# A multimodal attention block: the first block's scale as a column from TensorE, reordered transposes, and output tiles of 512, 512 and 128 columns

## Chip, core and metric

The kernel runs on one core of a Trainium2 chip. Its time is device microseconds of one execution, and lower is better. The profile is one execution taken by the hardware profiler; its times count from the start of the span.

## The reference, cut to what matters

```python
mod_i = (silu(c) @ wmod_img).reshape(B, 6, 1, D)       # B 2, D 1152
shi, sci, gai = mod_i[:, 0], mod_i[:, 1], mod_i[:, 2]
hi = layernorm(x_img) * (1 + sci) + shi                # x_img (2, 256, 1152)
qkvi = hi @ wqkv_img
...                                                    # the same for 32 text tokens per batch
p = softmax(einsum('bqd,bkd->bqk', q, k) * D ** -0.5)  # text and image tokens together
out_i = x_img + gai * ((p @ v)[:, Nt:] @ wo_img)
out_t = x_txt + gat * ((p @ v)[:, :Nt] @ wo_txt)
```

The first matrix product that keeps TensorE busy for long is V of the image. It needs the normalised image, transposed, times the scale column (1 + sci) of each block of 128 features. So four things must be there before it starts: the image, the scale weight (2.65 MB), the transposes, and the first piece of the V weight.

## The kernel before: the parts concerned

The scale is computed as rows: the scale weight is the moving operand, and `silu(c)` is loaded as 32 weight columns at four places of the array. VectorE then transposes the result to columns (`sc_cols`). The transposed image goes through PSUM tiles `tp`, three blocks each; ACT (ScalarE) or VectorE copies them out. `mm` and `tr` are TensorE's product and transpose, and `pin` keeps an instruction at its place in program order.

```python
ps_mm = tile_pool(name="ps_mm", bufs=6, space=PSUM)
ps_tr = tile_pool(name="ps_tr", bufs=2, space=PSUM)
...
def x_transposes(k0, b):
    tr_pool = b == 1 or k0 < 6                  # b 0, k0 6 takes a tile of ps_mm
    tp = (ps_tr if tr_pool else ps_mm).tile([P, 3, NI], bf, ...)
    for kt in range(k0, k0 + 3):
        for t in range(TPB):                    # TPB 2: the two token tiles of a batch
            i = b * TPB + t
            tr(tp[:, kt - k0, t * P:(t + 1) * P], xn_i[:, i, kt * P:(kt + 1) * P], ident[:])
    ...                                         # returns the copy to xT_i: VectorE for k0 3, else ACT
...
for out in [x_transposes(k0, 0) for k0 in (0, 3, 6)]:
    out()
sc_rows(0, 4)                                   # first piece of the scale weight
warm_up(3)
sc_rows(4, 7)                                   # second piece
out01 = x_transposes(0, 1)
out31 = x_transposes(3, 1)
sc_rows(7, K8)                                  # third and fourth pieces
sc_rows(K8, KT)
out61 = x_transposes(6, 1)
out01()
sc_cols(0, 1)                                   # VectorE: rows to a column
x_scale(0, 1, 0, step=1)                        # VectorE: first scaled block
sc_cols(1, 5)
x_scale(1, 3, 0)
v_open(A0, 0, 3)                                # V begins
...
def out_img(i, chunks, parts=None, between=None):
    for n in chunks:                            # (384, 384, 384); last tile (384, 384, 224, 160)
        if c0 and between: between = between()  # tile 1: the text gate, after its first chunk
        ...                                     # nine products of n columns
        nc.vector.tensor_mul(tmp[:, 0:n], ps[:, 0:n], gb[:, b, c0:c0 + n])
        nc.vector.tensor_add(o[:, c0:c0 + n], tmp[:, 0:n], x_i[:, i, c0:c0 + n])
```

Of the kernel before, what the change touches and what calls it, by code (L numbers as in the profile page):

```python
# [14 lines left out]
def kernel(  # L15
# [14 lines left out]
    nc = tc.nc  # L30
    bf = mybir.dt.bfloat16
    f32 = mybir.dt.float32
    PSUM = bass.MemoryType.PSUM

    B, NI, D = x_img.shape
    NT = x_txt.shape[1]
    P = 128
    KT = D // P
    NTOK = NI + NT
    NIT = (B * NI) // P  # L40
    TPB = NI // P
    NTT = B * NT
    CH = 384
    NCH = D // CH
    VC = 288
# [7 lines left out]
    work = ctx.enter_context(tc.tile_pool(name="work", bufs=2))  # L53
    small = ctx.enter_context(tc.tile_pool(name="small", bufs=4))
    ps_mm = ctx.enter_context(tc.tile_pool(name="ps_mm", bufs=6, space=PSUM))
    ps_tr = ctx.enter_context(tc.tile_pool(name="ps_tr", bufs=2, space=PSUM))

    pin = tc.keep_in_program_order

    def mm(*a, **k):  # L60
        return pin(nc.tensor.matmul(*a, **k))  # L61

    def tr(*a, **k):
        return pin(nc.tensor.transpose(*a, **k))  # L64
# [6 lines left out]
    x_i = act.tile([P, NIT, D], bf)  # L71
# [4 lines left out]
    def wtile(slot):  # L76
        return wpool.tile([P, KT, D], bf, tag="w%d" % slot, name="t")
# [4 lines left out]
    K8 = KT - 1  # L82
# [17 lines left out]
    w_sc_i = wtile(0)  # L100
# [21 lines left out]
    warm = const.tile([P, 512], bf)  # L122
# [3 lines left out]
    unit = const.tile([P, LW], bf)  # L126
# [5 lines left out]
    def warm_up(n):  # L132
        for _ in range(n):
            mm(wps[:], lhsT=warm[:, 0:P], rhs=warm[:], start=True, stop=True)
# [33 lines left out]
    sT = const.tile([P, KT, B], bf)  # L168
# [42 lines left out]
    def ln_norm(x_ap, mean, rstd, np_, out_ap):  # L211
        pin(nc.vector.tensor_scalar(out_ap, x_ap, mean, rstd[0:np_, :], op0=ALU.subtract, op1=ALU.mult))

    xn_i = act.tile([P, NIT, D], bf, tag="A")
    hS_i = act.tile([P, KT, B * NI], bf, tag="Bt")
    xT_i = act.tile([P, KT, B * NI], bf)
# [3 lines left out]
    def group(w, kt, g):  # L220
        return w[:, kt, :].rearrange("p (c g l) -> p g c l", g=NGG, l=LW)[:, g]

    def mod_cols_of(gps, name):
        t = const.tile([P, KT, LW], f32, name=name, tag={"sctc": "shc"}.get(name, name))
        pin(nc.vector.transpose(t[:].rearrange("p c l -> p (c l)"), gps[:].rearrange("p c l -> p (c l)")))
        return t

    sc_ps = ps_mm.tile([P, KT, LW], f32, tag="mm")

    def sc_rows(r0, r1):  # L230
        if r0 == 0:
            for g in range(NGG):
                mm(sc_ps[LW * g:LW * g + LW].rearrange("p c l -> p (c l)"), lhsT=unit[:], rhs=warm[:, 0:KT * LW],
                   start=True, stop=False, tile_position=(0, LW * g))
        for kt in range(r0, r1):
            for g in range(NGG):
                mm(sc_ps[LW * g:LW * g + LW], lhsT=sT32[:, kt, :], rhs=group(w_sc_i, kt, g),
                   start=False, stop=(kt == KT - 1), tile_position=(0, LW * g))

    def x_transposes(k0, b):  # L240
        tr_pool = b == 1 or k0 < 6
        tp = (ps_tr if tr_pool else ps_mm).tile([P, 3, NI], bf, tag="tr" if tr_pool else "mm", name="tp")
        for kt in range(k0, k0 + 3):
            for t in range(TPB):
                i = b * TPB + t
                tr(tp[:, kt - k0, t * P:(t + 1) * P], xn_i[:, i, kt * P:(kt + 1) * P], ident[:])
        dst = xT_i[:, k0:k0 + 3, b * NI:(b + 1) * NI]

        def copy_out():
            pin(nc.vector.tensor_copy(dst, tp[:]) if k0 == 3 else nc.scalar.copy(dst, tp[:]))  # L250

        return copy_out

    sc1_i = const.tile([P, KT, LW], f32, name="scc", tag="scc")

    def sc_cols(c0, c1):
        pin(nc.vector.transpose(sc1_i[:, c0:c1, :].rearrange("p c l -> p (c l)"),
                                sc_ps[:, c0:c1, :].rearrange("p c l -> p (c l)")))

    def x_scale(k0, k1, b, step=TPB):  # L260
        for kt in range(k0, k1):
            for t in range(0, TPB, step):
                t0, t1 = b * NI + t * P, b * NI + (t + step) * P
                pin(nc.vector.tensor_scalar(hS_i[:, kt, t0:t1], xT_i[:, kt, t0:t1], sc1_i[:, kt, b:b + 1], None,  # L264
                                            op0=ALU.mult))

    VW = 512
# [3 lines left out]
    def v_open(ids, k0, k1, kt_major=True):  # L271
        for key in ids:
            if key not in accs:
                accs[key] = ps_mm.tile([P, VW], f32, tag="mm", name="vps")
        loop = [(kt, key) for kt in range(k0, k1) for key in ids] if kt_major else \
            [(kt, key) for key in ids for kt in range(k0, k1)]
        for kt, (i, cc) in loop:
            mm(accs[(i, cc)][:], lhsT=hS_i[:, kt, i * P:(i + 1) * P], rhs=w_v_i[:, kt, cc * VW:(cc + 1) * VW],
               start=(kt == 0), stop=(kt == KT - 1), skip_group_check=True)
            if kt == KT - 1:  # L280
                evac(v_i[:, i, cc * VW:(cc + 1) * VW], accs[(i, cc)][:])
# [18 lines left out]
    r3, r2 = ln_rstd(m3[:, 1:2], P), ln_rstd(s2[:, 2:3], P, sign=-1.0)  # L300
    ln_norm(x_i[:, 3, :], m3[:, 0:1], r3, P, xn_i[:, 3, :])
    ln_norm(x_i[:, 2, :], s2[:, 0:1], r2, P, xn_i[:, 2, :])
    for out in [x_transposes(k0, 0) for k0 in (0, 3, 6)]:
        out()
    sc_rows(0, 4)
    warm_up(3)
    sc_rows(4, 7)
    out01 = x_transposes(0, 1)
    out31 = x_transposes(3, 1)
    sc_rows(7, K8)  # L310
    sc_rows(K8, KT)
    out61 = x_transposes(6, 1)
    out01()
    sc_cols(0, 1)
    x_scale(0, 1, 0, step=1)
    sc_cols(1, 5)
    x_scale(1, 3, 0)
    v_open(A0, 0, 3)
    out31()
    out61()  # L320
    x_scale(0, 3, 1)
    sc_cols(5, KT)
    for k0 in (3, 6):
# [200 lines left out]
    gb = act.tile([P, B, D], bf, tag="Bt")  # L524
    gbf = act.tile([P, 2, VC], bf)
    xf = act.tile([P, 2, VC], bf)
# [112 lines left out]
    def attn_pair(ids0, ids1):  # L639
        t0 = {key: ps_mm.tile([P, NTOK], f32, tag="mm", name="aps") for key in ids0}  # L640
        attn_keys(t0, True)
        t1 = {key: ps_mm.tile([P, NTOK], f32, tag="mm", name="aps") for key in ids1}
        for n, key in enumerate([x for pair in zip(t0, t1) for x in pair]):
            first, (b, dt) = key in t1, key
            r0, vcols = v_txt_cols(b, dt)
            mm((t1 if first else t0)[key][:], lhsT=vcols,
               rhs=pTs[b][r0:r0 + NT, 2, :], start=first, stop=not first, tile_position=(r0, 0))
        attn_evac(t0)
        attn_keys(t1, False)
        attn_evac(t1)  # L650
# [34 lines left out]
    for dts in ((0, 5, 1), (6, 2, 7), (3, 8, 4)):  # L685
        attn_pair(*[[(b, dt) for dt in dts] for b in range(B)])

    def out_img(i, chunks, parts=None, between=None):
        b = i // TPB
        t0 = b * NTOK + qpos[b][i % TPB]  # L690
        o = work.tile([P, D], bf, tag="o")
        c0 = s0 = 0
        for n in chunks:
            if c0 and between:
                between = between()
            ps = ps_mm.tile([P, CH], f32, tag="mm")
            for dt in range(KT):
                mm(ps[:, 0:n], lhsT=aT[:, dt, t0:t0 + P], rhs=w_o_i[:, dt, c0:c0 + n],
                   start=(dt == 0), stop=(dt == KT - 1))
            tmp = work.tile([P, CH], bf, tag="tmp")  # L700
            nc.vector.tensor_mul(tmp[:, 0:n], ps[:, 0:n], gb[:, b, c0:c0 + n])  # L701
            nc.vector.tensor_add(o[:, c0:c0 + n], tmp[:, 0:n], x_i[:, i, c0:c0 + n])  # L702
            c0 += n
            if parts is None and c0 == D or parts and c0 in parts:
                (nc.scalar if parts and c0 == D else nc.sync).dma_start(oi_v[b, i % TPB, :, s0:c0], o[:, s0:c0])
                s0 = c0

    def out_txt():
        of = work.tile([P, 2, VC], bf, tag="of", bufs=1)
        for r in range(2):  # L710
            ps = ps_mm.tile([P, VC], f32, tag="mm")
            for dt in range(KT):
                for g in range(2):
                    c0 = (2 * r + g) * VC
                    mm(ps[64 * g:64 * g + NTT, :], lhsT=aT[:, dt, NI:NI + NTT], rhs=w_o_t[:, dt, c0:c0 + VC],
                       start=(dt == 0), stop=(dt == KT - 1), tile_position=(0, 64 * g))
            tmp = work.tile([P, CH], bf, tag="tmp")
            nc.vector.tensor_mul(tmp[:, 0:VC], ps[:], gbf[:, r, :])
            nc.vector.tensor_add(of[:, r, :], tmp[:, 0:VC], xf[:, r, :])
        for g in range(2):  # L720
            eng = nc.sync if g == 0 else nc.scalar
            eng.dma_start(ot_flat.rearrange("t (r g j) -> g t r j", r=2, g=2)[g], of[64 * g:64 * g + NTT, :, :])

    C3 = (CH, CH, CH)
    out_img(0, C3)
    out_img(1, C3, between=txt_gate)
    out_img(2, C3)
    out_txt()
    out_img(3, (CH, CH, 224, 160), parts=(2 * CH, D - 160, D))


# [28 lines left out]
```

## Time and profile before

| | before |
|---|---|
| time, median of 3 runs | 118.11 us (117.92 to 118.4) |
| TensorE busy, share of the span | 95% |
| first product of the second scale piece | 11.70 us |
| first V product | 14.15 us |
| last VectorE addition starts | 113.27 us |

The last two rows are read from the chain in order of time; the stretch between them is 99.12 us and holds nearly nothing but TensorE. What can be changed at the start lies ahead of 14.15 us. The prediction shows the lines for it. Three more are of use. Two are from the timeline of TensorE: start, length, what, count.

```profile
12.96 0.51 PE L61 MATMUL sc_ps<-t,sT 128*32 128x288 bf16 x8
13.58 0.49 PE L64 MATMUL tp<-ident,xn_i 128*128 128x128 bf16 x6
```

The last six transposes begin at 13.58 because their tile is the one that ACT empties until 13.53. The third is from VectorE's timeline near the end; the bracket is the idle time ahead and what ended it.

```profile
108.43 0.46 DVE L718 TENSOR_TENSOR tmp<-ps,gbf 128x288 bf16<-128x288 f32 x1 [1.41 <-PE ps L61]
```

This is the text output times its gate `gbf`, which comes through a small round trip to memory.

### The profile page before, as it was taken

The page shows a single profiled execution, that of the slowest core. Times are in us where ns is not written, and L with a number is a line of the kernel's source. Part 1 is how long each engine was busy: PE and PEld are TensorE (multiplying, and loading weights), DVE is VectorE, ACT ScalarE, POOL GpSimd, SP SyncE. Part 2 cuts the span into 40 slices and gives each one's busy share as a digit, 9 for nine tenths or more (in the row PEclk, how much of TensorE's full clock was granted, in tenths as well). Part 3 has the DMA queues.
Part 4 walks back from the last instruction along what each step waited for, and adds up shares of the span by engine and source line. Part 5 has one row for each costly group of instructions (what it writes and reads, how often), then busy time and mean ns, then how long its engine had stood idle before and what let it go on. Part 6 is the DMA issues. An engine that isn't in the chain of part 4 may idle for free.

```text
span 116.0 us, 2561 instructions
## 1 busy us (share of the span) xinstructions
PE 110.5 (95%) x1064; PEld 63.6 (55%) x1072; DVE 72.2 (62%) x153; ACT 44.3 (38%) x92; POOL 12.4 (11%) x34
## 2 busy tenths in 40 slices
PE   4999999999999999999999999999999999999990
PEld 1246644445674444444454457887866565566670
DVE  3478594062869999999995040018758508566571
ACT  4799710041752298725241233244657400100000
POOL 7300000000000000000000000003440700407000
PEclk9999999999999999999999999999999999999999
DMA  3999999999999999999999999999999999931323
GB/s 111 373 373 404 406 405 408 416 411 408 416 398 408 319 408 410 405 412 412 411 340 412 412 412 414 402 416 400 412 403 409 409 415 366 363 139 37 116 51 102
DMA packets 18917, 41.02 MB, mean 354 GB/s; under 512 B 1323, under 2 KB 1851, under 8 KB 18907
## 3 DMA queue, kind: packets, MB, share of 16 engines
q1 hardware_dynamic: 18032, 39.85, 89.4%
q0 software_dynamic: 480, 0.89, 2.3%
q10 hardware_dynamic: 395, 0.12, 0.4%
q8 instruction: 8, 0.13, 0.4%
q14 instruction: 2, 0.02, 0.0%
HBM read 39.52 MB, written 1.34 MB: 352 GB/s over the span
## 4 chain that ended last, share of the span: by engine, by line
PE 84%; DMA 8%; DVE 2%; SPq 1%; issue 1%; ACT 1%; DVEq 0%
PE ps L61 52%; PE vps L61 15%; DMA t<-in_wmod_img_dram 8%; PE gps L61 5%; PE aps L61 5%; PE sps L61 4%; DVE tmp L701 1%; PE sc_ps L61 1%; DVE o L702 1%; SPq L104 1%; PE tp L64 1%; ACT pT L621 1%; PE pT_ps L64 0%; SPq L108 0%; PE tpt L64 0%
## 5 line engine op out<-in xcount | busy, mean ns | idle before, releaser
L61 PE MATMUL ps<-xT_i,t 128*128 128x512 bf16 x157 | 35.4, 379 | 0.3
L61 PEld LDWEIGHTS <-t 128*128 128x128 bf16 x324 | 20.5, 98 | 19.0 <-issue 0.5
L435 DVE SCALAR_TENSOR_TENSOR acc_sh<-t,sTf,acc_sh 128x1152 f32<-128x1152 bf16 x16 | 21.4, 1404 | 0.0
L61 PE MATMUL ps<-t,aT 128*128 128x384 bf16 (+3 forms) x153 | 20.3, 308 | 0.0
L61 PE MATMUL vps<-t,hS_i 128*128 128x512 bf16 (+1 forms) x106 | 17.8, 325 | 0.2
L61 PEld LDWEIGHTS <-aT 128*128 128x128 bf16 (+1 forms) x153 | 13.0, 101 | 7.1 <-issue 0.8
L61 PEld LDWEIGHTS <-hS_i 128*128 128x128 bf16 x108 | 9.0, 98 | 8.7 <-DVE hS_i L264 0.4
L365 ACT CAST qkT<-ps 128x512 bf16<-128x512 f32 (+2 forms) x11 | 6.1, 551 | 15.0 <-PE ps L61 13.6
L701 DVE TENSOR_TENSOR tmp<-ps,gb 128x384 bf16<-128x384 f32 (+2 forms) x13 | 6.8, 524 | 7.2 <-DMA gb<-mod_scratch 3.8
L587 POOL TENSOR_SCALAR pb<-e,rs 128x32 bf16<-128x32 f32 (+1 forms) x5 | 2.2, 445 | 76.0 <-DVE rs L584 76.0
L61 PE MATMUL wps<-warm 128*128 128x512 bf16 x24 | 8.1, 499 | 1.6 <-DVE unit L127 1.5
L363 ACT ACTIVATE qkT<-ps 128x512 bf16<-128x512 f32 (+2 forms) x11 | 6.1, 561 | 8.6 <-PE ps L61 8.5
L180 DVE CAST v_i<-vps 128x512 bf16<-128x512 f32 x5 | 3.5, 691 | 7.5 <-PE vps L61 7.5
L572 DVE TENSOR_REDUCE nmx<-sps 128x1 f32<-128x288 f32 x4 | 1.8, 458 | 9.5 <-PE sps L61 9.5
L182 ACT CAST v_i<-vps 128x512 bf16<-128x512 f32 x4 | 2.3, 580 | 9.9 <-PE vps L61 9.9
L61 PEld LDWEIGHTS <-sT 128*32 128x32 bf16 x180 | 4.6, 96 | 2.4 <-issue 1.8
L61 PEld LDWEIGHTS <-warm 128*128 128x128 bf16 x25 | 2.7, 118 | 5.5 <-issue 3.0
L634 DVE TENSOR_SCALAR aT<-aps,svc 128x288 bf16<-128x288 f32 x9 | 4.3, 518 | 2.2 <-PE aps L61 2.2
L61 PE MATMUL sps<-qkT 128*128 128x288 bf16 (+1 forms) x54 | 5.3, 287 | 0.0
L61 PE MATMUL gps<-t,sT 128*32 128x288 bf16 x144 | 5.2, 287 | 0.0
L61 PE MATMUL ps<-hT_t,t 128*128 128x64 bf16 x162 | 5.2, 193 | 0.0
L61 PE MATMUL aps<-pT,v_i 128*128 128x288 bf16 x36 | 5.1, 287 | 0.1
(111 smaller groups left out, 105.3 us busy)
## 6 DMA issues: line engine op xcount, KB each, us to landing
t<-in_wqkv_txt_dram SPq DMA_DIRECT2D x3, 2592.0 KB, 19.1
t<-in_wmod_img_dram SPq DMA_DIRECT2D x2, 2592.0 KB, 14.1
t<-in_wmod_txt_dram SPq DMA_DIRECT2D x2, 2592.0 KB, 18.1
t<-in_wqkv_img_dram SPq DMA_DIRECT2D x3, 864.0 KB, 14.0
t<-in_wqkv_img_dram SPq DMA_DIRECT2D x1, 2592.0 KB
t<-in_wo_img_dram SPq DMA_DIRECT2D x3, 864.0 KB, 9.8
t<-in_wqkv_img_dram SPq DMA_DIRECT2D x3, 576.0 KB, 10.0
t<-in_wmod_txt_dram SPq DMA_DIRECT2D x2, 864.0 KB, 13.1
```

The costliest lines, as they stand in the source:

```text
L61: return pin(nc.tensor.matmul(*a, **k))
L64: return pin(nc.tensor.transpose(*a, **k))
L104: nc.sync.dma_start(x_i[:, b * TPB:(b + 1) * TPB, :], x_img[b].rearrange("(p t) d -> p t d", t=TPB))
L180: nc.vector.tensor_copy(out_ap, in_ap)
L182: nc.scalar.copy(out_ap, in_ap)
L363: nc.scalar.mul(out_ap, in_ap, SCALE)
L365: nc.scalar.copy(out_ap, in_ap)
L435: pin(nc.vector.scalar_tensor_tensor(acc, w_sh_t[:, kt, :], col, acc, op0=ALU.mult, op1=ALU.add))
L572: pin(nc.vector.reduce_max(nmx[0:qn, :], sps[0:qn, :], axis=AX.X, negate=True))
L587: pin(nc.gpsimd.tensor_scalar(pb[0:qn, NI + 2 * NT:NI + 3 * NT], e[0:qn, NI:NTOK], rs[0:qn, :], 0.0, op0=ALU.mult, op1=ALU.add))
L634: nc.vector.tensor_scalar(dst, tiles[(b, dt)][:], bias, None, op0=ALU.add)
L701: nc.vector.tensor_mul(tmp[:, 0:n], ps[:, 0:n], gb[:, b, c0:c0 + n])
```

## The change

There are three intents. The first block's scale is computed a second time as a column, so that V need not wait for eight row products and VectorE's transpose. Six transposes of batch 1 move ahead of the second weight piece, to fill TensorE's wait for it. The output chunks become 512 columns wide where they had 384. The core of the diff:

```diff
+    sc0_ps = ps_mm.tile([P, B], f32, tag="mm")
+    tp60 = ps_mm.tile([P, 3, NI], bf, tag="mm", name="tp")
+    tp61 = ps_mm.tile([P, 3, NI], bf, tag="mm", name="tp")     # k0 6 of both batches
+    def sc_first(r0, r1):
+        if r0 == 0:
+            mm(sc0_ps[:], lhsT=warm[:, 0:P], rhs=unit[:, 0:B], start=True, stop=False)
+        for kt in range(r0, r1):
+            mm(sc0_ps[:], lhsT=w_sc_i[:, kt, 0:P], rhs=sT[:, kt, :], start=False, stop=(kt == KT - 1))
 ...
     sc_rows(0, 4)
-    warm_up(3)
+    sc_first(0, 4)
+    warm_up(2)
+    t0, t3, t6 = [(x_tiles(k0, 1), k0, 1) for k0 in (0, 3, 6)]
+    x_transposes(*t0, ts=(1,))
+    x_transposes(*t3, ts=(1,))
     sc_rows(4, 7)
-    out01 = x_transposes(0, 1)
-    out31 = x_transposes(3, 1)
-    sc_rows(7, K8)
-    sc_rows(K8, KT)
-    out61 = x_transposes(6, 1)
-    out01()
-    sc_cols(0, 1)
-    x_scale(0, 1, 0, step=1)
-    sc_cols(1, 5)
+    sc_first(4, 7)
+    x_transposes(*t0, ts=(0,))
+    x_transposes(*t3, ts=(0,))
+    x_transposes(*t6)
+    sc_first(7, K8)
+    sc_first(K8, KT)
+    sc_rows(7, KT)
+    x_out(*t0)
+    x_out(*t6)
+    x_scale(0, 1, 0, step=1, first=True)      # scale read from sc0_ps
+    sc_cols(0, 5)
 ...
+            pin(nc.vector.tensor_mul(...)); pin(nc.vector.tensor_add(...))
-    C3 = (CH, CH, CH)
+    C3 = (OW, OW, D - 2 * OW)                  # OW 512
-    out_img(3, (CH, CH, 224, 160), parts=(2 * CH, D - 160, D))
+    out_img(3, (OW, 256, 224, 160), parts=(2 * CH, D - 160, D))
```

More of the change, by code (lines that the diff above doesn't have):

```diff
@@ L238, in sc_rows, with x_tiles, x_transposes, x_out @@
                    start=False, stop=(kt == KT - 1), tile_position=(0, LW * g))
-    def x_transposes(k0, b):
-        tr_pool = b == 1 or k0 < 6
-        tp = (ps_tr if tr_pool else ps_mm).tile([P, 3, NI], bf, tag="tr" if tr_pool else "mm", name="tp")
+    def x_tiles(k0, b):
+        return (tp61 if b else tp60) if k0 == 6 else ps_tr.tile([P, 3, NI], bf, tag="tr", name="tp")
+    def x_transposes(tp, k0, b, ts=range(TPB)):
         for kt in range(k0, k0 + 3):
-            for t in range(TPB):
+            for t in ts:
                 i = b * TPB + t
                 tr(tp[:, kt - k0, t * P:(t + 1) * P], xn_i[:, i, kt * P:(kt + 1) * P], ident[:])
+    def x_out(tp, k0, b):
         dst = xT_i[:, k0:k0 + 3, b * NI:(b + 1) * NI]
-        def copy_out():
-            pin(nc.vector.tensor_copy(dst, tp[:]) if k0 == 3 else nc.scalar.copy(dst, tp[:]))
-        return copy_out
+        pin(nc.vector.tensor_copy(dst, tp[:]) if k0 == 3 else nc.scalar.copy(dst, tp[:]))
     sc1_i = const.tile([P, KT, LW], f32, name="scc", tag="scc")
@@ L258, in sc_cols, with x_scale @@
                                 sc_ps[:, c0:c1, :].rearrange("p c l -> p (c l)")))
-    def x_scale(k0, k1, b, step=TPB):
+    def x_scale(k0, k1, b, step=TPB, first=False):
         for kt in range(k0, k1):
@@ L263, in x_scale @@
                 t0, t1 = b * NI + t * P, b * NI + (t + step) * P
-                pin(nc.vector.tensor_scalar(hS_i[:, kt, t0:t1], xT_i[:, kt, t0:t1], sc1_i[:, kt, b:b + 1], None,
+                pin(nc.vector.tensor_scalar(hS_i[:, kt, t0:t1], xT_i[:, kt, t0:t1],
+                                            sc0_ps[:, b:b + 1] if first else sc1_i[:, kt, b:b + 1], None,
                                             op0=ALU.mult))
@@ L302 @@
     ln_norm(x_i[:, 2, :], s2[:, 0:1], r2, P, xn_i[:, 2, :])
-    for out in [x_transposes(k0, 0) for k0 in (0, 3, 6)]:
-        out()
-    sc_rows(0, 4)
-    warm_up(3)
-    sc_rows(4, 7)
-    out01 = x_transposes(0, 1)
-    out31 = x_transposes(3, 1)
-    sc_rows(7, K8)
-    sc_rows(K8, KT)
-    out61 = x_transposes(6, 1)
-    out01()
-    sc_cols(0, 1)
-    x_scale(0, 1, 0, step=1)
-    sc_cols(1, 5)
+    tps = [(x_tiles(k0, 0), k0, 0) for k0 in (0, 3, 6)]
+    for tp in tps:
+        x_transposes(*tp)
+    for tp in tps:
+        x_out(*tp)
+    sc_rows(0, 4)
+    sc_first(0, 4)
[3 more added lines that the diff above has]
+    x_transposes(*t3, ts=(1,))
+    sc_rows(4, 7)
+    sc_first(4, 7)
[9 more added lines that the diff above has]
+    sc_cols(0, 5)
     x_scale(1, 3, 0)
     v_open(A0, 0, 3)
-    out31()
-    out61()
+    x_out(*t3)
     x_scale(0, 3, 1)
@@ L686 @@
         attn_pair(*[[(b, dt) for dt in dts] for b in range(B)])
+    OW = 512
     def out_img(i, chunks, parts=None, between=None):
@@ L695, in out_img @@
                 between = between()
-            ps = ps_mm.tile([P, CH], f32, tag="mm")
+            ps = ps_mm.tile([P, OW], f32, tag="mm")
             for dt in range(KT):
@@ L699, in out_img @@
                    start=(dt == 0), stop=(dt == KT - 1))
-            tmp = work.tile([P, CH], bf, tag="tmp")
-            nc.vector.tensor_mul(tmp[:, 0:n], ps[:, 0:n], gb[:, b, c0:c0 + n])
-            nc.vector.tensor_add(o[:, c0:c0 + n], tmp[:, 0:n], x_i[:, i, c0:c0 + n])
+            tmp = work.tile([P, OW], bf, tag="tmp")
+            pin(nc.vector.tensor_mul(tmp[:, 0:n], ps[:, 0:n], gb[:, b, c0:c0 + n]))
+            pin(nc.vector.tensor_add(o[:, c0:c0 + n], tmp[:, 0:n], x_i[:, i, c0:c0 + n]))
             c0 += n
@@ L716, in out_txt @@
                        start=(dt == 0), stop=(dt == KT - 1), tile_position=(0, 64 * g))
-            tmp = work.tile([P, CH], bf, tag="tmp")
-            nc.vector.tensor_mul(tmp[:, 0:VC], ps[:], gbf[:, r, :])
-            nc.vector.tensor_add(of[:, r, :], tmp[:, 0:VC], xf[:, r, :])
+            tmp = work.tile([P, OW], bf, tag="tmp")
+            pin(nc.vector.tensor_mul(tmp[:, 0:VC], ps[:], gbf[:, r, :]))
+            pin(nc.vector.tensor_add(of[:, r, :], tmp[:, 0:VC], xf[:, r, :]))
         for g in range(2):
```

## The prediction

> **What bounds the kernel now.** I read the page first: shares of busy time, then the chain of waits. TensorE is busy nearly throughout, its clock is granted in full, and the chain that ended last lies on it for 84%, with one transfer of the first weight for 8%.
>
> ```profile
> PE 110.5 (95%) x1064; PEld 63.6 (55%) x1072; DVE 72.2 (62%) x153; ACT 44.3 (38%) x92; POOL 12.4 (11%) x34
> PE 84%; DMA 8%; DVE 2%; SPq 1%; issue 1%; ACT 1%; DVEq 0%
> ```
>
> Next the chain in order of time. It shows where TensorE stops being late for data and becomes the bound itself.
>
> ```profile
> 2.12 9.54 DMA t<-in_wmod_img_dram
> 11.66 0.04 issue
> 11.70 0.55 PE sc_ps L61 x12
> 12.25 0.78 PE tp L64 x12
> 13.03 0.46 PE sc_ps L61 x8
> ...
> 13.51 0.23 DVE scc L257
> ...
> 13.83 0.27 DVE hS_i L264
> 14.10 0.05 issue
> 14.15 2.12 PE vps L61 x9
> ```
>
> Until 11.66 us the second piece of the scale weight is on its way. Then come row products of that weight, twelve transposes, eight more row products, VectorE's transpose of the scale to columns, the first scaled block (hS_i) and, at 14.15, the first V product. From 14.15 to 111.4 the same view is TensorE work with only 0.05 us issue gaps and one 0.65 us ACT copy; a table by stage gives TensorE 98.30 busy of 98.85 us from 14.15 to 113. So **a delay or gain of the V start passes to the end nearly one for one**, and a gain elsewhere counts only if it shortens TensorE's stream or the last VectorE steps.
>
> The timeline of ACT and VectorE around the start carries my main step:
>
> ```profile
> 11.14 2.39 ACT L250 COPY xT_i<-tp 128x768 bf16<-128x768 bf16 x3
> 11.34 0.57 DVE L212 TENSOR_SCALAR xn_i<-x_i,sm,rstd 128x1152 bf16<-128x1152 bf16 x1
> 11.83 0.55 DVE L250 COPY xT_i<-tp 128x768 bf16<-128x768 bf16 x1
> 12.19 0.84 PE L64 MATMUL tp<-ident,xn_i 128*128 128x128 bf16 x12
> ```
>
> These copies empty batch 0's transpose tiles. ACT's first ends near 11.94 (2.39 over three copies) and frees one of the two buffers of the transpose pool; VectorE's ends at 11.83 + 0.55 = 12.38 and frees the other. Before, batch 1's transposes begin at 12.19, behind the row products, and reach the second buffer only after it is free.
>
> **What the Trainium skill says.** (1) TensorE: Matmul & The Clock Gate, Part 2, on LDWEIGHTS: matmuls stay in program order, only weight loads are pulled ahead. So a matmul that waits for a buffer holds everything behind it. The trace agrees in kind: the loads for batch 1's last six transposes begin at 13.39, their matmuls at 13.58, when ACT's third copy (to 13.53) frees their tile. (2) The same page, Back-to-back issue gap: N/2.4 + 2.5 ns when isolated, but about 131 ns for N=512 sustained. Here the V and Q streams take 1.945 us per nine 512-column products (evacuations at 36.49, 38.44, 40.38), or 216 ns; nine of 384 take 1.465 us (VectorE's tail steps at 100.22, 101.68, 103.15), or 162.8. The trace agrees with the formula and not with the 131 ns. (3) PSUM — Partial Sum Buffer, the four PSUM rules: one product fills at most one bank of 512 fp32 columns. So a 512-column tile needs no more banks than a 384-column one, and six buffers stay six; no number here tests it. (4) VectorE: DVE Perf Modes, perf-mode tier table: two-tensor operations go at single rate from PSUM, double from bf16 SBUF. The tail products take 557 ns at 384 columns and 324 at 160, 1.04 ns a column; the additions 358 and 241, 0.52 a column. It agrees.
>
> **The change part by part.**
>
> *Scale column.* It adds ten small products (one opener, nine with two columns); five lie after the second weight piece. A load with a 64-column product takes 47 ns here (88 in 4.17 us), so I take 45 ns each, an estimate: 0.23 us after 11.66. In return the first scaled block no longer waits for eight row products and a VectorE transpose. Before, from 13.03 that was 0.46 + 0.04 + 0.23 + 0.09 = 0.80 us to the scaling at 13.83. After, two small products of 0.09 plus about 0.17 to drain: 0.26. On its own **this path shortens by some 0.55 us**. But the eight row products still precede V in TensorE's order (the listing of the built program confirms it), about 0.33 us (41 ns each, from 12 between 11.70 and 12.19). V start is then the later of scaling and row products.
>
> *The last six transposes* get their own tile, so they no longer wait from about 13.29 to 13.58. Before, that wait lay beside VectorE's path: they ended at 14.07 and V began at 14.15. It removes something that was nearly equal in length to the critical path.
>
> *The reordering* moves six transposes ahead of the second weight piece's row products, to use idle TensorE time. The row they need is normalised by 10.85 + 0.58 = 11.43, but their target tiles are not free. The built program shows the first waiting for ACT and the fourth for VectorE. So, from the durations above, with 64 ns per transpose (12 in 0.77):
>
> - first three: 11.97 to 12.16; next three: wait to 12.43, done 12.62;
> - twelve row products, 0.49: 13.11; three small products: 13.25;
> - twelve transposes, 0.77: 14.02; two small products issued by 14.11, drained 14.26;
> - first scaling 14.28 + 0.27 = 14.55; row products issued by 14.44;
> - **V starts near 14.60**, against 14.15: +0.45 us.
>
> The weight piece that was waited for before (11.66) is now there 0.96 us before its first use: the wait has become a buffer wait. VectorE keeps up afterwards: the columns for blocks 0 to 4 at about 14.70 to 15.05, block 1 scaled by 15.36, wanted at 14.60 + 4 x 0.216 = 15.46. That is only 0.1 us of slack.
>
> *One warm-up product fewer* (0.21 us) lies in idle time: 0.
>
> *Output chunks.* Columns and number of products per tile stay: 1152 and 27. TensorE should take equally long, but 128-column products cost a little more than the formula: nine of 512 and 36 of 128 took 4.06 us together (29.13 to 33.19), so (4.06 - 1.945)/36 = 59 ns against 53.3 + 2.8. That is 3 ns x 27 products in three tiles = +0.09 us. VectorE's sum is linear in columns with the same number of steps, so also unchanged: 3 x (0.557 + 0.358) = 2.75 us before; by the slopes 2 x (0.69 + 0.43) + 0.29 + 0.23 = 2.76 after. The **pinning** alters no order: the listing shows the same sequence. 0.
>
> *Text gate.* It is computed after the first chunk of the second output tile, now 512 columns: 128 x 9 / 2.4 = 0.48 us later. Its transfers end near 108.3 (last issue 106.26 plus 2.0), and the text product on VectorE begins at 108.43 although TensorE had it ready near 107.2: so it waited for that transfer, whatever the table of waits names. It will now begin 0.48 later relative to TensorE. VectorE then reaches the last tile's first chunk at about 110.45, when TensorE delivers it (108.48 + 1.945 = 110.43), and catches up in the 256-column chunk with 0.15 us to spare. 0, at most +0.1.
>
> *Final chunk.* Before, the 224-column step began at 112.30, both when VectorE was free and when TensorE was ready (111.43 + 0.865). The smaller second chunk frees VectorE earlier, but TensorE still rules:
>
> ```profile
> 112.30 0.39 DVE L701 TENSOR_TENSOR tmp<-ps,gb 128x224 bf16<-128x224 f32 x1
> 112.72 0.28 DVE L702 TENSOR_TENSOR o<-tmp,x_i 128x224 bf16<-128x224 bf16 x1
> 112.91 0.32 DVE L701 TENSOR_TENSOR tmp<-ps,gb 128x160 bf16<-128x160 f32 x1
> ```
>
> Gain 0 to 0.02. Sum: +0.45 + 0.09 = +0.54.
>
> **The rivals.** *(a) The intent succeeds:* V starts up to 0.3 us earlier. For it speaks that the VectorE hop falls away; the limit is the first V weight, issued at 3.74 and landed 10.1 later, 13.84. It needs the moved transposes to find free tiles before 12; VectorE's copy at 11.83 to 12.38 speaks against it. Time 117.8. *(b) The buffer wait replaces the weight wait,* as worked out: 118.6. *(c) The text gate's transfers become the tail's bound:* they are slow small transfers (4.8 us for 2.2 KB), and the slack is 0.15 us; a late one would add 0.2 to 0.5, to about 119. *(d) The scale read from PSUM slows VectorE,* or block 1 misses its 0.1 us slack: +0.1, inside the range.
>
> **Range and chances.** (b) weighs 65%, (a) 25%, because these start times come from one trace and overlaps of 0.2 us can be missed; the rest for (c). I put the centre a little under (b): **118.5 us, 117.8 to 119.1**, run spread of before being 117.92 to 118.4. A 2% change is 2.4 us, and the whole stretch changed at the start, 11.66 to 14.15, is no longer than that: faster 0.01, same 0.97, slower 0.02.
>
> **What would show it.** The batch 1 transposes: three near 11.97, three near 12.43, with TensorE idle ahead of each; if all six are done by 11.9, (b) is wrong. First V product near 14.60. The first scaling near 14.28, with no VectorE transpose before it. Nine 128-column products in about 0.53 us. The text gate product on VectorE 0.48 us later against TensorE's output stream. No DMA wait before the second weight piece. Wrong most easily: the copies or normalisations falling earlier than in this trace, or the scaling being later than TensorE's own queue.

## The result and the profile after

The changed kernel took 118.64 us in the median of 6 runs (118.12 to 118.71), the kernel before 118.31 beside it (117.92 to 118.45). The ratio is 1.0026, with a 95% interval of 1.0002 to 1.0049. All ratios here are the mean time of one kernel's fast runs over that of the other's fast runs of the same rounds, so they are not quite the ratios of the medians.

The chain's shares by engine show what starts it now:

```profile
PE 84%; ACT 5%; DMA 3%; DVE 3%; issue 1%; DVEq 0%
```

The 8% that was the second piece of the scale weight is gone. In its place stand the image's landing (3%) and ACT's passes over it (5%). The chain in order of time shows the hand-over; columns are start, length, what:

```profile
11.08 1.07 DVE xn_i L212 x2
12.14 0.48 DVE xT_i L260
12.62 0.04 issue
12.66 0.33 PE tp L64 x3
12.99 0.64 PE sc_ps L61 x15
13.63 0.69 PE tp L64 x12
14.33 0.06 PE sc_ps L61 x2
...
14.48 0.27 DVE hS_i L272
14.75 0.05 issue
14.80 1.25 PE vps L61 x5
```

VectorE's copy of batch 0's second tile (xT_i, to 12.62) now releases three transposes (12.66), and everything after them follows in TensorE's order: row products, twelve transposes, two small products, the scaling, V. VectorE's transpose of the scale has left this chain, as intended. The timeline of TensorE names the first of the two buffer waits, and that of VectorE the copy that makes the second:

```profile
12.20 0.79 PE L64 MATMUL tp<-ident,xn_i 128*128 128x128 bf16 x6 [0.76 <-ACT xT_i L260]
```

```profile
12.06 0.55 DVE L260 COPY xT_i<-tp 128x768 bf16<-128x768 bf16 x1
```

TensorE sat idle for 0.76 us ahead of the first; for 0.54 of it, from 11.66 on, the row to transpose was normalised (11.08 + 0.58), and it waited only for ACT to empty the target. The end of the kernel is unchanged in length. VectorE's timeline there:

```profile
101.70 0.69 DVE L720 TENSOR_TENSOR tmp<-ps,gb 128x512 bf16<-128x512 f32 x1 [1.75 <-PE ps L61]
...
104.14 0.69 DVE L720 TENSOR_TENSOR tmp<-ps,gb 128x512 bf16<-128x512 f32 x1 [0.84 <-PE ps L61]
...
106.08 0.69 DVE L720 TENSOR_TENSOR tmp<-ps,gb 128x512 bf16<-128x512 f32 x1 [0.79 <-PE ps L61]
...
107.81 0.46 DVE L737 TENSOR_TENSOR tmp<-ps,gbf 128x288 bf16<-128x288 f32 x1
108.31 0.31 DVE L738 TENSOR_TENSOR of<-tmp,xf 128x288 bf16<-128x288 bf16 x1
108.92 0.46 DVE L737 TENSOR_TENSOR tmp<-ps,gbf 128x288 bf16<-128x288 f32 x1 [0.30 <-PE ps L61]
```

Steps that wait for TensorE are a clock for TensorE. From 104.14 to 106.08 it made 512 columns nine times (1.94 us), and from 101.70 to 104.14 a 128-column chunk and a 512-column one (2.44 us), so nine 128-column products take 0.50 us, 55.6 ns each. The text step at 107.81 has no wait of its own in this trace, against 1.41 us before.

**A ruler for all traces.** Two arrivals differ from trace to trace whatever the kernel: that of the first half of the image, seen as ACT's first pass over it, and that of the second scale piece, seen as its first product where TensorE is already waiting for it (before, e2, e3, e5). There the DMA queue of SyncE issues its next transfer 0.02 to 0.03 us ahead of that product; this issue stands in every trace's timeline (`--engine SP`), so it gives the piece's landing for the other kernels too. So I read every V start from both arrivals. All times are in us; "end" is the start of the last VectorE addition. The labels are those of the experiments below.

| kernel | ACT's first pass | second piece landed (SyncE's next issue) | second piece's first product | V starts | V less ACT's pass | V less piece | end less V |
|---|---|---|---|---|---|---|---|
| before | 4.52 | 11.67 | 11.70 | 14.15 | 9.63 | 2.45 | 99.12 |
| after | 4.76 | 11.72 | 12.92 | 14.80 | 10.04 | 1.88 | 98.99 |
| r_after_again | 4.74 | 12.11 | 12.91 | 14.79 | 10.05 | 1.88 | 98.98 |
| e1_lead_only | 4.42 | 12.27 | 12.59 | 14.46 | 10.04 | 1.87 | 98.99 |
| e2_output_only | 4.75 | 12.02 | 12.05 | 14.48 | 9.73 | 2.43 | 99.07 |
| e3_order_back | 4.70 | 12.32 | 12.35 | 14.56 | 9.86 | 2.21 | 98.98 |
| e4_free_tile | 4.61 | 11.58 | 11.84 | 13.88 | 9.27 | 2.04 | 98.99 |
| e4_again | 4.87 | 11.61 | 12.10 | 14.14 | 9.27 | 2.04 | 98.99 |
| e5_column_only | 4.72 | 11.87 | 11.90 | 14.19 | 9.47 | 2.29 | 98.98 |
| e6_reorder_only | 4.80 | 11.29 | 12.97 | 15.35 | 10.55 | 2.38 | 99.22 |
| e7_free_tile_late | 4.78 | 11.71 | 12.02 | 13.91 | 9.13 | 1.89 | 99.14 |
| e7_again | 4.79 | 11.72 | 12.02 | 13.99 | 9.20 | 1.97 | 99.14 |

Three things can be read off. The changed kernel's start is 10.04 us behind ACT's pass in three traces, although ACT's pass itself moves by 0.34. The start of before is 2.43 to 2.45 behind the weight piece's first product in the two traces that have it (before, e2). And from V on, all kernels need 98.98 to 99.22 us: what is gained or lost is gained or lost ahead of V, but for 0.2 us.

The landing lets one trace stand for two kernels. With the start of before, V would come 0.03 + 2.45 us after it: an estimate of 14.20 in the trace of after, where V started at 14.80, of 14.59 against 14.79 in r_after_again, and of 14.75 against 14.46 in e1. **The same start loses 0.6 us, loses 0.2 or gains 0.3 by which of the two arrivals is late.** A third arrival, the first V weight, sets a floor: by issue and time to landing it lands at 13.6 to 14.5 in these traces.

### The profile page after: what moved, and what is told of

Read it like the earlier page. It is cut to its first block, busy times and chain, and to the rows that moved or that the text cites. A ratio compares the mean times of both kernels' runs of the same rounds, so it can differ in the third digit from the quotient of the medians.

```text
span 116.5 us, 2574 instructions
## 1 busy us (share of the span) xinstructions
PE 109.5 (94%) x1069; PEld 62.3 (54%) x1081; DVE 71.8 (62%) x152; ACT 44.1 (38%) x92; POOL 12.4 (11%) x34
## 4 chain that ended last, share of the span: by engine, by line
PE 84%; ACT 5%; DMA 3%; DVE 3%; issue 1%; DVEq 0%
PE ps L61 53%; PE vps L61 15%; PE gps L61 5%; PE aps L61 5%; PE sps L61 4%; DMA x_i<-in_x_img_dram 3%; ACT xn_i L197 2%; ACT xn_i L198 2%; DVE xn_i L212 1%; PE tp L64 1%; PE sc_ps L61 1%; DVE tmp L720 1%; ACT pT L638 1%; ACT rstd L207 1%; ACT rstd L208 1%
## 5 line engine op out<-in xcount | busy, mean ns | idle before, releaser
L61 PE MATMUL ps<-t,aT 128*128 128x512 bf16 (+5 forms) x150 | 20.2, 306 | 0.2
L61 PEld LDWEIGHTS <-aT 128*128 128x128 bf16 (+1 forms) x153 | 12.0, 101 | 8.1 <-issue 0.5
L720 DVE TENSOR_TENSOR tmp<-ps,gb 128x512 bf16<-128x512 f32 (+4 forms) x13 | 6.8, 523 | 8.3 <-PE ps L61 4.6
L61 PE MATMUL wps<-warm 128*128 128x512 bf16 x23 | 7.0, 460 | 1.5 <-DVE unit L127 1.5
```

The source lines that it names most:

```text
L61: return pin(nc.tensor.matmul(*a, **k))
L720: pin(nc.vector.tensor_mul(tmp[:, 0:n], ps[:, 0:n], gb[:, b, c0:c0 + n]))
```

## The experiments

Theory A: the moved transposes wait for tiles that are still being emptied and hold up the row products behind them, while the column is a gain and the output chunks are neutral. The rivals: the output chunks or the later text gate cost the time; the small products, or a scale read from PSUM, cost it; or a later landing of the image is all there is.

**Start alone.** The changed kernel with 384-column chunks.

```diff
-    OW = 512
+    OW = CH
-    C3 = (OW, OW, D - 2 * OW)
+    C3 = (CH, CH, CH)
-    out_img(3, (OW, 256, 224, 160), ...)
+    out_img(3, (CH, CH, 224, 160), ...)
```

> The changed kernel's start with the 384-column output chunks of before. If the loss comes from the start alone (theory A: the moved transposes wait for their tiles), the time stays at the changed kernel's 118.6 us, +0.3 on before, with the V start at 14.6 to 14.8 us. If the output chunks or the later text gate carry the loss (rival), it falls to that of before, 118.3.

Measured: 118.38 us (118.25 to 118.74), ratio to before 0.9991 (0.9965 to 1.0016). By the time alone this speaks for the rival: it did not stay at +0.3. The trace says otherwise. Its V start is again 10.04 behind ACT's pass, only that pass came early (4.42), and from V to the end it needs the same 98.99 us as the changed kernel. The time was a miss of my expectation: this kernel came 0.2 us lower and before was slower in this job (118.56). The image was early here and the weight piece late (12.27), which favours this start. The chain of this trace goes back to the first V weight, which landed at 14.42; but the scaling began 0.32 us ahead of V, as in the changed kernel (14.14 to 14.46, 14.48 to 14.80), so the weight added nothing to speak of.

**Output alone.** The start of before with the new chunks and pinned steps.

```diff
-            ps = ps_mm.tile([P, CH], f32, tag="mm")
+            ps = ps_mm.tile([P, OW], f32, tag="mm")             # OW 512
-            nc.vector.tensor_mul(...); nc.vector.tensor_add(...)
+            pin(nc.vector.tensor_mul(...)); pin(nc.vector.tensor_add(...))
-    C3 = (CH, CH, CH)
+    C3 = (OW, OW, D - 2 * OW)
-    out_img(3, (CH, CH, 224, 160), ...)
+    out_img(3, (OW, 256, 224, 160), ...)
```

> The start of before with the changed kernel's 512-512-128 chunks and pinned VectorE steps. Theory A: same as before, 118.3, within 0.1 (my prediction had charged +0.09 for the 128-column products; the trace of the changed kernel suggests 0). Rival: +0.3.

Measured: 118.67 us (118.02 to 119.25), ratio 1.0011 (0.9976 to 1.0047). The interval excludes neither; the trace does better: 99.07 us from V to the end against 99.12 before, and the 0.05 lies in the text products discussed last, not in the output. **In these traces the new chunks cost nothing and give nothing.**

**The order put back.**

```diff
-    x_transposes(*t0, ts=(1,))
-    x_transposes(*t3, ts=(1,))
     sc_rows(4, 7)
     sc_first(4, 7)
-    x_transposes(*t0, ts=(0,))
-    x_transposes(*t3, ts=(0,))
+    x_transposes(*t0)
+    x_transposes(*t3)
     x_transposes(*t6)
```

> The changed kernel with the six moved transposes put back behind the second weight piece's products; scale column, own tile for the last six and output chunks stay. Theory A: the wait for the two tiles goes, V starts near 14.05 us instead of 14.60 to 14.80, time 0.5 us below the changed kernel, near 118.1. Rivals (a later landing of the image, the scale read from PSUM, the extra small products): no change, 118.6.

Measured: 118.29 us (117.5 to 118.44), ratio 0.9964 (0.9931 to 0.9996). The V start was 14.56, half a microsecond later than expected, because the second piece landed at 12.30 in this trace. The chain in order of time:

```profile
2.12 10.18 DMA t<-in_wmod_img_dram
12.31 0.04 issue
12.35 0.71 PE sc_ps L61 x15
13.06 1.03 PE tp L64 x18
```

The chain starts from the weight again, no longer from ACT's pass and the copies: the buffer wait is gone. V is 2.21 behind the weight, against 2.45 before, so what remains of the change is a gain of 0.24 us at the start. Nothing of the column or the chunks was touched, so the rivals of the small products and of the image's landing do not carry the loss. This rests on the trace: with the changed kernel's distance V would have come at 4.70 + 10.04 = 14.74 here. By time alone this kernel is only 0.09 us under the start alone of the same job (118.38), and their runs overlap.

**Transposes moved ahead into a free tile.** Of the changed kernel, three transposes go ahead instead of six: those of the last group, whose tile is free from the start.

```diff
-    x_transposes(*t0, ts=(1,))
-    x_transposes(*t3, ts=(1,))
+    x_transposes(*t6, ts=(1,))
     sc_rows(4, 7)
     sc_first(4, 7)
-    x_transposes(*t0, ts=(0,))
-    x_transposes(*t3, ts=(0,))
-    x_transposes(*t6)
+    x_transposes(*t0)
+    x_transposes(*t3)
+    x_transposes(*t6, ts=(0,))
```

> The changed kernel with three transposes moved ahead, those of the last group, whose tile is free from the start, instead of six whose tiles are not. Theory A: they run at about 11.45 to 11.65 us in idle time, nothing waits, V starts near 13.9 us, where the first V weight lands (13.84), 0.7 us below the changed kernel, 117.9. If moving transposes ahead costs in itself: not below the kernel with the order put back.

Measured: 117.93 us (117.61 to 118.28), ratio 0.9946 (0.992 to 0.9973). TensorE's timeline:

```profile
11.57 0.34 PE L64 MATMUL tp<-ident,xn_i 128*128 128x128 bf16 x3 [0.27 <-DVE xn_i L212]
11.84 0.55 PE L61 MATMUL sc_ps<-t,sT 128*32 128x288 bf16 x12
```

The transposes now wait for the normalised row (DVE xn_i), which is a real need, and not for a copy. V starts at 13.88, 9.27 behind ACT's pass instead of 10.04. **So it was not moving transposes ahead that cost, but moving those whose tiles were taken.** The edit also moves three transposes instead of six; that the wait went with the tile and not with the number is shown by the releaser, DVE xn_i here and ACT xT_i there, and not by the time.

> The version with three transposes of the free tile moved ahead, once more, since it is the one offered as better than both: again 0.993 to 0.997 of before, and V starting 9.27 us after ACT's first pass over the image unless the first V weight lands later than that.

Measured: 118.06 us (117.73 to 118.8), ratio 0.9993 (0.9964 to 1.0022). The distance is 9.27 again, but the ratio expected was missed: the image came late (pass at 4.87, V at 14.14) and before was quick in this job (118.18). So the gain over before is not settled by these two.

**The changed kernel once more**, because the first two jobs seemed to disagree.

> The changed kernel once more, because it was +0.26% on before in one job and its start alone -0.09% in another. In the traces the V start of before follows the landing of the second weight piece (2.45 us after the first product that needs it), and that of the changed kernel follows ACT's first pass over the image (10.04 us later). Expected: the same two distances (2.45 and 10.04) here, and a time from equal to before to +0.3, by which of the two arrivals was late on this chip.

Measured: 118.70 us (118.17 to 118.73), ratio 1.0016 (0.9988 to 1.0043). V starts 10.05 behind ACT's pass; the 2.45 of before could not be seen here, since a job does not keep the trace of before. Together with the first job: **slower by 0.2 to 0.3%, with one interval that excludes equality and one that does not.** The start alone, which differs only in its chunks, was at 0.9991 in its job.

**The column alone**, in the order and the tiles of before.

```diff
+    sc0_ps = ps_mm.tile([P, B], f32, tag="mm")       # and sc_first, x_scale(first=) as in the change
     sc_rows(0, 4)
-    warm_up(3)
+    sc_first(0, 4)
+    warm_up(2)
     sc_rows(4, 7)
+    sc_first(4, 7)
     ...                                              # transposes as before
-    sc_rows(7, K8)
-    sc_rows(K8, KT)
+    sc_first(7, K8)
+    sc_first(K8, KT)
+    sc_rows(7, KT)
     ...
-    sc_cols(0, 1)
-    x_scale(0, 1, 0, step=1)
-    sc_cols(1, 5)
+    x_scale(0, 1, 0, step=1, first=True)
+    sc_cols(0, 5)
```

> Before with only the scale column added: order of the transposes, their tiles and the output as before. Theory A (the column is a gain, the reordering is the loss): V starts 2.25 to 2.35 us after the first product of the second weight piece instead of 2.45, since the last six transposes still wait for ACT's third copy; time 0.1 to 0.3 us below before. If the column's ten extra products cost as much as they save: equal to before.

Measured: 118.11 us (117.93 to 118.28), ratio 0.9976 (0.9949 to 1.0002, so equality is just inside), and V 2.29 behind the weight piece, as expected. TensorE's timeline shows why it is no more:

```profile
13.85 0.49 PE L64 MATMUL tp<-ident,xn_i 128*128 128x128 bf16 x6
14.19 1.89 PE L61 MATMUL vps<-t,hS_i 128*128 128x512 bf16 x7
```

The scaling ran at 13.61, but TensorE still had the last six transposes in front of V.

**The reordering alone**, without the column.

```diff
-    sc_first(0, 4)
-    warm_up(2)
+    warm_up(3)
     ...                                              # moved transposes and their tiles as in the change
-    sc_first(4, 7)
     ...
-    sc_first(7, K8)
-    sc_first(K8, KT)
-    sc_rows(7, KT)
+    sc_rows(7, K8)
+    sc_rows(K8, KT)
     ...
-    x_scale(0, 1, 0, step=1, first=True)
-    sc_cols(0, 5)
+    sc_cols(0, 1)
+    x_scale(0, 1, 0, step=1)
+    sc_cols(1, 5)
```

> The changed kernel without the scale column: the reordering and the own tile stay, the first block again takes its scale through eight row products and VectorE's transpose. Theory A: V starts 10.5 us after ACT's first pass over the image instead of 10.04, time 0.4 to 0.5 above the changed kernel, 0.5 to 0.9 above before. If the column gave nothing here: equal to the changed kernel.

Measured: 119.05 us (118.88 to 119.28), ratio 1.0051 (1.0023 to 1.0078), which is 0.35 us above the changed kernel of the same job, a little less than expected. V starts 10.55 behind ACT's pass:

```profile
14.23 0.43 PE L61 MATMUL sc_ps<-t,sT 128*32 128x288 bf16 x8
15.35 0.82 PE L61 MATMUL vps<-t,hS_i 128*128 128x512 bf16 x3 [0.69 <-DVE hS_i L266]
```

Here TensorE waits 0.69 us for VectorE's transpose and scaling, the hop that the column removes. So **the two halves of the change at the start pull against each other: the column gives 0.5 us of V start where the reordering exposes it, and the reordering takes more than that.**

**A further step: three transposes behind the first V products.** On the version with the free tile:

```diff
-    x_transposes(*t6, ts=(0,))
 ...
-    x_out(*t6)
 ...
-    v_open(A0, 0, 3)
+    v_open(A0, 0, 1)
+    x_transposes(*t6, ts=(0,))
+    x_out(*t6)
+    v_open(A0, 1, 3)
```

> The better version (three transposes of the free tile moved ahead) with the other three of that tile put behind the first four V products. Expected: V starts up to 0.19 us earlier than in the version with the free tile (9.27 after ACT's first pass), unless the first V weight, landed at 13.84 to 14.42, is what it then waits for. Time 117.8 to 117.95 against before's 118.3, thus 0.994 to 0.996 of before.

Measured: 117.85 us (117.53 to 118.3), ratio 0.9955 (0.9925 to 0.9985). V starts at 13.91, and its chain now goes back to the V weight: issued at 4.25, landed 9.62 later, at 13.87. This is the floor that the prediction named. Repeated:

> The version with three transposes of the free tile ahead and three behind the first V products, once more, because its sister measured 0.9946 of before in one job and 0.9993 in another. V should start 9.1 us after ACT's first pass over the image or when the first V weight lands, whichever is later; time 0.994 to 0.999 of before, and below 118.3 in the median on any chip.

Measured: 118.01 us (117.79 to 118.59), ratio 0.9984 (0.9949 to 1.0019); V at 13.99, 9.20 behind ACT's pass where 9.1 was expected, because the first V weight landed only at 13.94 (issued at 4.24, 9.7 to landing). This version and its sister without the last step were below before in the median in all four of their comparisons, by 0.1 to 0.5%, but two of the four intervals include equality. In the one job that held both, this version took 117.85 us and the changed kernel 118.70. So **it beats the changed kernel more surely than it beats before.** Its V start stands at the landing of the first V weight, so a next step would have to bring that weight sooner; no run here tries it.

**A tenth of a microsecond in the text products.** From V to the end the kernels without the column need 99.07 to 99.22 us, those with it 98.98 to 98.99 (leaving aside the one that puts transposes among its V products). The difference lies in one place, the 81 products of the text keys: 2.66 us before, 2.60 with the new output, 2.76 with the reordering alone, 2.52 after. Two looks separate two possible reasons, the place in the PSUM pool and the number of TensorE instructions ahead.

```diff
 # one tile more in the pool
+    spare = ps_mm.tile([P, B], f32, tag="mm")
+    mm(spare[:], lhsT=warm[:, 0:P], rhs=unit[:, 0:B], start=True, stop=True)
     warm_up(3)
 # 18 TensorE instructions more, no tile more
+    for _ in range(10):
+        mm(wps[:, 0:B], lhsT=warm[:, 0:P], rhs=unit[:, 0:B], start=True, stop=True)
-    warm_up(3)
+    warm_up(2)
```

> Before with one more tile taken from the PSUM pool ahead of the scale rows, written by one two-column product and never read, so that every later tile moves on by one buffer. In all traces with the scale column, the K products of the text queries' stage take 4.04 us; without it 4.12 to 4.32. If the place in the pool does it: 4.04 here. If the number of TensorE instructions ahead does it: 4.12 or more.

> Before with ten small products more and one warm-up product fewer at the place of the scale column's first ones, all into the warm-up tile, so that TensorE has 18 instructions more and the tiles stay where they were. If the number of instructions ahead does it: 4.04 us for that stage of the text K products. If the place in the pool does it: 4.12 or more.

Measured, the row of these 81 products in TensorE's timeline, with the spare tile and with the spare instructions:

```profile
73.60 2.70 PE L61 MATMUL ps<-hT_t,t 128*128 128x64 bf16 x81
```

```profile
73.75 2.53 PE L61 MATMUL ps<-hT_t,t 128*128 128x64 bf16 x81
```

From V to the end they need 99.16 and 98.99 us; as times they took 118.38 and 118.44, one run each. So of these two the short form goes with the instruction count and not with the pool. The count cannot be all: before, the new output alone and the reordering alone have the same number ahead and took 2.66, 2.60 and 2.76 us. Why a count should matter is left open.

## Why the prediction was right

The measured 118.64 us lies in the range of 117.8 to 119.1 and near the 118.5 given; it was the second rival, the buffer wait in place of the weight wait, that came true. The range would also have held the first rival's 117.8, so it is the timeline and not the time that tells them apart. That the time came within 0.14 us of the number is partly luck: before was measured at 118.31 beside it, not at the 118.11 that the prediction started from, and against it the change is worth +0.31 us, not +0.54. By its own steps:

- **The buffer wait: right, to the size.** Predicted were three transposes near 11.97 and three near 12.43 with V at 14.60. That was counted from a trace in which ACT's pass began at 4.52, so 10.08 behind it; measured were 10.04, 10.05 and 10.04. In the trace the transposes came at 12.20 and 12.66 and V at 14.80, all 0.2 later with the image. Inside the chain small errors cancelled: the second three transposes took 0.26 us and not 0.19, the three small products 0.09 and not 0.14, the twelve transposes 0.66 and not 0.77, and from the last two small products to the scaling it was 0.32 and not 0.26. Putting the order back removed the wait, and moving transposes of a free tile instead made V 0.77 us earlier against ACT's pass (10.04 to 9.27).
- **The column: right in direction, its extra products over-sized.** I charged 45 ns for each. In the timeline of after, three of them separate 13.41 from the next transpose at 13.50, so about 30. The 47 ns that it came from divided a row of the chain that mixes the 64-column products with some of 512 columns; by the timeline of the same trace 81 of them fill 73.35 to 75.84, so 31 each. The gain of "some 0.55 us on its own path" showed as 0.51 where nothing else hid it (10.55 less 10.04) and as 0.16 in the order of before (2.45 less 2.29), where the last transposes follow.
- **The sum: too large, by its smaller terms.** +0.54 was worked out from one trace. It left out that before's V start follows the weight piece and the new one follows the image, and both move. Over all 14 traces (the table, and the two looks with ACT's pass at 4.69 and 4.48 and the landing at 11.92 and 12.13) ACT's pass came at 4.69 in the mean and the weight piece's landing, read from SyncE's queue, at 11.85. So, as an estimate from these means (the landing's is uncertain by 0.08), V comes at 4.69 + 10.04 = 14.73 against 11.85 + 0.03 + 2.45 = 14.33: +0.40, near the +0.45 predicted for V. The +0.09 for the chunks was not there, and 0.13 came back in the text products, which the prediction did not have: +0.27. The two measured ratios are worth +0.31 and +0.19 us.
- **The 128-column products: wrong, the one term of the sum that failed outright.** The +0.09 rested on V's 36 products at 59 ns. In the output they take 55.6 ns, and from V to the end the kernel takes 98.99 us with either chunking at the new start.
- **The text gate: wrong in the step, without effect.** VectorE's text product was to begin 0.48 us later against TensorE's stream. In the trace of after it did not wait at all: the gate's first round trip, from the write's issue to the read's, took 2.91 us (100.35 to 103.26) where it had taken 5.28 before (99.35 to 104.63). But it varies from trace to trace of one kernel: in r_after_again it took 3.95 (100.33 to 104.28), and the product, at 108.08, waited 0.41 us for the gate's transfer, with the same 98.98 us from V to the end. So the prediction's wait for that transfer is real in some traces; its added delay was not seen in either.
- **Pinning, warm-up and final chunk: nothing, as said.** No experiment changed them one by one; they are inside the two halves that were tested.
- **Block 1's slack and the scale read from PSUM: no loss.** VectorE's two first scalings take 0.42 us together before and after.

What stays open is how much slower the changed kernel is than before on a given chip: the arrivals move by more than the difference.

## What to carry to other kernels

Work can be moved into idle time only if its target buffer is free by then: look up who empties the buffer and when, not only when the input is ready, because TensorE's order makes everything behind the moved work wait as well. When arrivals race, read each start as a distance from the arrival that it follows: jobs that seem to contradict each other in the median can then be compared. And a shorter path to one consumer is worth only what the queue of that consumer leaves over: the column gave 0.5 us or 0.16 us by what stood ahead of V.

## What the Trainium skill lacked or had wrong

- TensorE: Matmul & The Clock Gate, Back-to-back issue gap, gives about 81 ns (N = 128) and 131 ns (N = 512) for sustained streams of load and product. The runs show 55.6 ns in the output chunks and 216 ns in the Q stream, which fit its formula for isolated products, N/2.4 + 2.5.
- The same section's table gives about 60 cycles, or 25 ns, as the floor for 1 to 64 columns, and about 62 ns with hardware decode off. Two-column products with a full 128-column load take about 30 ns here, which is near the first; 81 products of 64 columns take 29 ns each from start to start (74.00 to 76.36 in after), or 30 to 32 in some builds of the same stage.
- No page that I read tells of that difference, 2.52 against 2.60 to 2.76 us for the same 81 products; in one look the short form came with 18 TensorE instructions more far ahead. Runtime: NRT & Kernel Launch, Instruction fetch mechanics, says that TensorE's instructions come in blocks of 256 and that crossing a block costs little that shows; no run here tells whether that is the cause.
